# About 320 instructions at other places in the order of a Fourier-mixing and feed-forward kernel

## The chip, the cores and the metric

The kernel runs on one core of a Trainium2 chip. The metric is the device time of one execution in microseconds (us). The kernel before has a median of 676.51 us over three runs (675.86 to 678.52). Engines are named as in the profile: PE is TensorE, DVE is VectorE, ACT is ScalarE, POOL is GpSimd and SP is SyncE, which here only issues transfers.

## The reference

```python
a = einsum("bsd,ed->bse", LN(x), dft_hid_re);  b = einsum("bsd,ed->bse", LN(x), dft_hid_im)
h = x + einsum("ts,bse->bte", dft_seq_re, a) - einsum("ts,bse->bte", dft_seq_im, b)
out = h + silu(LN(h) @ w1) @ w2
```

Everything is float32, with batch 1, sequence length S = 2048, model width D = 512 and inner width F = 1792. LN subtracts the mean over the model width and divides by the root of the variance plus 1e-5.

## The kernel before

**Arithmetic.** A float32 product is made of three matmuls in the reduced format fp32r. Each moving operand is split by `rounded` (L236 to L250): ScalarE copies it to a high part `ph` (L242), and VectorE subtracts that from the source and has the remainder `pl` (L246, or L248 where a sign is turned). `three` (L290) then issues the products high by high, high by remainder and low weight by high (L292, L293, L294). All matmuls of the large stages take 512 columns. On top of this, the matrix products are done in forms with seven block products in place of eight, so VectorE also adds and subtracts blocks of the operands (`sub` and `prep`, L694; the results in L717, L790 and L840).

**Stages, in order of time.** The mixing along the sequence comes first, as the product of the sequence matrices with x: `plain(0,0)` (profile names c, X, S; up to about 98 us), `fast(1,0)` (m; to 165), then the mixing along the width, `mix(0)` (y; to 209), for the first half of the rows. Then the second half: `fast(0,1)` (m; to about 290), `fast(1,1)` (to 365) and `mix_fast(1)` (y; to 404), whose weights hf are read back from DRAM: they were stored there as fd and ad by GpSimd. The feed-forward layer follows, `down` and `up` (y, vx, g, f, wf, sf), until 670. In between VectorE and ScalarE make sums of w1 and w2 (`sums_w1`, L1051 to L1073; `make_w2`, L1174 to L1194), which are stored to DRAM and read back.

**The second layer norm.** h lies with the model width on partitions, so its mean and variance are sums over partitions. `total` (L956) adds the two tiles of h (L959), folds the result (L960), and calls GpSimd's `partition_all_reduce` (L961); this is the "sum over partitions". `norm_h` (L964) uses it twice for each of four blocks of rows: mean, centering (L976), squares on ScalarE (L982), variance. The variance then takes a trip through DRAM to be spread over 128 partitions of 4: a store of 2 KB from GpSimd (`row`, L988, `tk<-v`), a read (`gather`, L993, `rs<-tk`), twelve small operations on VectorE that make one over the root (`root` and `finish`, from L996), a store (L1002), a broadcast read (`spread`, L1005). The scaling L1010 follows, and the store nd (L1015), which the feed-forward stage reads back as hn.

**What sets the order.** `program` (L224) lists pieces of work, here called events, each with a time in us on a model clock. `step` puts a group of matmuls at the clock and its preparations at fixed leads ahead of it; `at` puts single pieces. Events are numbered in the order in which the code lists them. The last statement sorts them, and here the table MOVED (L44 to L132) comes in: it gives an offset in us to the event of a number.

```python
def step(n, mm, before=(), after=()):
    t, end = clock[0], clock[0] + n * MM_US
    for lead, f in before:
        events.append((t - lead, 1, len(events), f))
    events.append((t, 2, len(events), mm))
    ...
return sorted(((t + MOVED.get(n, 0.0), at, n, f) for t, at, n, f in events), key=lambda v: v[:3])
```

`fnet_ffn_kernel` goes through the sorted list twice. The first time it only notes when each SBUF page of 4 KB a partition is taken and last used, and `Plan.places` gives each tile one of 51 places, always the one that by its model has been free longest. The second time it emits the instructions and holds each of the five engines to exactly this order. So all engines work in order, SyncE's and GpSimd's transfers included: an instruction that waits holds back whatever stands behind it on its engine. A tile that takes a place also waits for the last users of the place, a store's landing among them.

**The events that the text names.** Each event here is written as its number.

- 369: matmuls of `mix(0)` (y, H10), before the next group. 376 and 389: loads of h from in_xT (L784), two halves each. 378: the first add h = y + h (L790), for which the matmuls of 425 wait. 380: the four sums hs of the second mixing matrix (L806).
- 431, 435, 440, 427, 448, 444: high parts on ScalarE; their remainders on VectorE are 432, 436, 441, 428, 449, 445. In the same way 462, 466, 470, 474, 498, 521, 551, 656, 664 are remainders of stage m; 477 is a sum of raw blocks (L694).
- 394 and 399: mean and variance of the first block of rows (two adds and the reduce each).
- 416 and 417: `root` and `finish` of the second block; 413, 414, 415 are its variance, `row` and `gather`.
- 684, 689, 694, 705, 710, 721: loads of hf for `mix_fast(1)` (two halves each); 686, 690, 696, 707 are the matmuls that read the first four. 695: a load of h from in_xT for the add L840 at 385 us. 825 to 828: loads hn<-nd.

Of the kernel before, what the change touches and what calls it, by code (L numbers as in the profile page):

```python
# [45 lines left out]
    12: 25.37, 14: 18.68, 16: 23.49, 21: 2.24, 24: 5.1, 28: 5.71, 30: 7.61, 31: 5.41, 32: 6.75, 35: 4.85, 36: 5.08,  # L46
    38: -0.24, 39: 3.5, 40: 6.36, 41: 1.55, 42: 0.25, 46: 6.79, 48: 5.99, 49: 5.67, 50: 7.6, 52: 3.63, 53: -4.14,
    54: -3.75, 57: -12.95, 58: -5.94, 59: 1.25, 60: -5.22, 61: -1.51, 63: 5.5, 64: -0.99, 65: -1.09, 66: -2.09,
    67: -0.1, 68: -0.57, 69: -14.93, 71: -24.64, 72: -18.25, 73: -16.87, 74: -15.18, 76: -0.67, 78: -10.64, 79: -6.28,
    80: 0.77, 81: -13.68, 82: 4.24, 84: -21.06, 85: -10.81, 86: -13.29, 87: -10.28, 88: 2.24, 89: 1.74, 92: -10.56,  # L50
    93: -1.15, 95: -6.14, 96: 3.53, 97: 1.06, 98: -1.97, 99: -0.07, 100: 2.76, 102: 0.43, 104: -2.79, 107: -8.69,
    108: -26.49, 110: -14.81, 111: -25.35, 112: -9.3, 116: 11.02, 118: 0.67, 119: 0.78, 121: 7.29, 122: 5.12,
    123: 9.89, 126: 0.66, 127: -0.06, 129: 5.4, 130: 4.42, 131: 1.43, 132: -0.74, 134: 0.06, 135: 0.91, 137: -2.02,
    138: -29.74, 139: -9.64, 141: -2.52, 142: 1.4, 145: -0.73, 146: -3.2, 147: -5.13, 148: -4.71, 149: 3.43,
    150: 2.26, 151: 19.19, 152: -27.16, 153: -17.66, 155: 11.15, 156: 11.07, 157: 17.67, 158: 17.63, 159: 14.66,
    160: 28.77, 161: 25.8, 162: -2.9, 163: -3.39, 164: -1.57, 165: -6.08, 166: -8.22, 167: 1.79, 168: -0.32,
    169: -3.29, 170: 3.74, 171: 1.24, 172: -18.88, 173: -19.39, 174: -6.33, 175: -8.5, 176: -5.26, 178: -5.15,
    179: -6.23, 180: 10.12, 181: 25.57, 182: -9.29, 183: -2.31, 184: 0.88, 185: 3.16, 186: 1.11, 188: 7.51, 189: 8.76,
    190: 7.03, 191: 5.95, 192: -10.95, 193: -3.24, 194: 8.07, 195: 6.17, 196: 5.36, 197: -18.74, 198: -10.39,
    199: -13.03, 200: -11.78, 201: -10.15, 202: 21.78, 203: 12.22, 204: 24.11, 205: 25.08, 206: 23.81, 207: -6.82,  # L60
    208: -5.87, 209: 5.68, 211: 0.38, 212: 4.81, 213: 4.09, 215: -5.32, 216: -0.23, 217: 2.38, 219: -16.42, 220: 5.22,
    221: 3.05, 223: 10.17, 224: -45.37, 225: -0.53, 226: 4.81, 228: -3.03, 229: 1.98, 230: 6.64, 233: 0.33, 234: 4.63,
    236: -20.67, 237: -4.86, 238: 4.99, 240: 13.91, 241: -7.64, 242: -8.45, 243: -2.11, 245: -18.15, 246: -15.09,
    247: -13.55, 249: -6.13, 250: -0.11, 251: 4.03, 253: -1.71, 254: 3.79, 255: 5.2, 257: 2.94, 258: 2.67, 259: 0.5,
    260: 1.59, 261: 0.52, 262: 2.64, 263: -2.76, 265: 4.76, 266: 3.32, 268: 4.67, 269: 6.93, 271: 6.39, 272: 7.88,
    273: 0.53, 274: 5.4, 275: 6.15, 276: -4.5, 278: 6.09, 279: 5.88, 280: 2.15, 282: 7.93, 283: 6.61, 285: 0.49,
    286: 0.9, 288: 2.33, 289: 2.31, 290: 2.16, 291: 2.6, 292: 2.43, 293: -5.69, 295: 3.01, 296: 5.2, 297: 6.85,
    299: -1.02, 302: -1.88, 303: 2.15, 305: 3.89, 306: 2.84, 307: 4.94, 308: 6.65, 309: 5.48, 310: -1.13, 312: 2.89,
    313: 6.78, 314: 5.19, 315: 2.32, 317: -4.12, 318: -0.55, 320: 3.15, 321: 1.08, 322: 2.71, 324: 2.35, 325: 6.97,
    326: 5.14, 327: 7.74, 329: 2.18, 330: -8.74, 331: 0.45, 332: 2.59, 333: 7.04, 334: 5.42, 335: -4.49, 338: 4.22,  # L70
    339: -12.19, 341: -15.7, 342: -18.67, 343: 1.36, 344: 2.27, 345: -2.79, 346: 2.6, 347: 2.51, 349: -4.7,
    350: -8.47, 351: -8.67, 352: 5.03, 353: 4.15, 354: -8.94, 355: 5.74, 356: 3.9, 357: 2.04, 358: -10.25, 360: -8.8,
    361: -4.61, 362: 0.81, 363: -0.42, 364: -0.7, 365: -1.32, 367: -4.56, 368: -3.92, 370: -9.58, 371: -5.5,
    372: -1.35, 373: 1.07, 374: -4.23, 375: -2.53, 376: 10.74, 378: 1.53, 379: 21.82, 380: -2.37, 381: -4.43,
    382: -1.85, 383: 9.92, 384: 12.54, 385: -3.96, 386: 19.12, 387: -5.64, 388: -2.68, 389: 6.11, 391: 2.25,
    392: 31.21, 393: 0.94, 394: -3.65, 395: -5.08, 396: -0.67, 397: 0.45, 398: -2.83, 399: -3.69, 400: -4.78,
    401: 3.37, 402: -1.34, 403: 0.17, 404: 5.79, 405: 8.49, 406: 2.76, 407: 6.66, 408: -27.67, 409: -5.26,
    410: -16.78, 411: -4.87, 412: -13.16, 413: -9.84, 416: 8.66, 417: 7.28, 418: 6.58, 419: 9.04, 420: 3.27,
    421: 8.16, 422: -3.11, 423: -3.82, 424: 0.47, 426: -23.77, 427: 3.56, 428: 6.96, 430: -16.19, 431: -11.09,
    432: -4.29, 434: -62.45, 435: 5.72, 436: 5.45, 439: -9.52, 441: 0.73, 444: -6.34, 445: -2.57, 447: -24.54,  # L80
    448: 2.95, 449: 2.53, 451: 1.94, 452: 3.93, 453: 5.93, 455: 11.48, 456: -5.77, 457: 6.32, 458: 6.74, 460: 5.56,
    461: 7.28, 462: 7.53, 464: 5.91, 465: 6.89, 466: 7.05, 468: -5.85, 469: -1.48, 470: 4.72, 472: -2.37, 473: -2.75,
    474: -1.83, 475: 0.43, 477: -0.58, 478: -2.17, 480: 1.69, 481: -0.48, 484: 6, 486: 5.62, 487: 5.35, 488: 5.34,
    489: 4.77, 490: 5.95, 491: 6.35, 493: 2.22, 494: 2.29, 495: -3.07, 497: -1.61, 498: 5.03, 500: 5.02, 501: 3.02,
    503: 5.25, 504: 4.47, 505: 1.31, 506: 1.52, 507: 2.32, 510: 6.63, 511: 5.94, 512: 9.73, 514: 5.45, 515: 5.04,
    517: -0.39, 518: 7.97, 520: 8.23, 521: 6.1, 522: 1.82, 523: 4.52, 524: 5.7, 525: -3.12, 527: 8.59, 528: 5.79,
    529: 3.62, 530: 7.7, 536: 4.91, 537: 3.2, 539: 2.32, 540: 6.62, 541: 6.7, 542: 8.33, 544: 9.12, 545: -33.8,
    546: 4.76, 547: 1.6, 548: 26.61, 549: -27.35, 550: -18.8, 551: -16.59, 554: 4.38, 555: 4.21, 558: 3.97, 559: 4.8,
    561: -9.81, 562: -5.24, 563: -6.01, 566: -6.52, 567: 4.31, 568: 4.51, 570: -20.73, 571: 0.57, 572: 0.31,
    575: -0.89, 576: 0.73, 578: -0.15, 579: 4.17, 580: 2.07, 582: 12.19, 583: 5.44, 584: 2.64, 585: 4.63, 587: -12.47,  # L90
    589: 2.94, 591: -11.64, 592: -5.78, 593: -7.73, 596: 6.89, 597: 5.63, 600: -3.91, 601: 3.55, 602: -6.54,
    603: -2.43, 604: -1.8, 605: -13.08, 607: -7.33, 608: 6.06, 610: -7.3, 614: 4.59, 615: -5.2, 616: -5.83,
    618: -8.39, 620: 8.96, 621: 7.18, 622: 6.56, 624: -1.21, 625: 3.84, 627: -8.97, 628: 5.64, 632: -4.62, 633: -5.73,
    634: -5.8, 635: -9.76, 637: 4.48, 638: 2.54, 639: 1.47, 642: 3.21, 644: 1.24, 645: 0.76, 647: -3.29, 648: -3.25,
    649: -12.3, 650: -8.36, 651: -1.12, 652: -19.86, 654: 3.38, 655: 3.83, 656: 2.17, 659: -14.33, 660: -13.59,
    663: -13.13, 664: -2.74, 666: 2.38, 667: 1.59, 668: 1.24, 669: 8.46, 672: -17.88, 673: -15.11, 674: -23.93,
    675: -34.26, 676: -17.44, 678: -28.28, 680: -19.6, 681: -3.67, 682: -8.48, 683: -1.66, 684: -18.81, 685: -5.98,
    687: -4, 688: -6.17, 692: -19.67, 693: -16.11, 694: 2.89, 695: 2.99, 697: 4.07, 698: 4.26, 699: -41.78, 701: 5.24,
    702: 4.58, 703: 4.51, 704: 7.6, 705: 3.1, 706: 17.25, 708: 1.9, 709: 1.31, 710: 2.94, 713: 1.55, 714: -20.76,
    716: -42.49, 717: -7.52, 719: -2.44, 721: -9.87, 723: 15.38, 724: -16.97, 728: 5.47, 730: 1.07, 731: 10.4,  # L100
    732: -3.37, 733: -0.27, 738: 12.29, 739: 13.87, 740: -42.3, 741: -31.4, 743: 2.11, 746: 4.55, 747: 9.34,
    748: 16.67, 749: 13.34, 750: 20.58, 751: 26.94, 752: 24.39, 753: 22.79, 754: 22.53, 755: 21.55, 756: 21.49,
    757: 26.94, 758: 47, 759: 32.53, 760: 38.11, 761: 39.91, 762: 13.17, 763: 13.96, 764: 16.64, 765: 14.1,
    766: 18.58, 767: 16.64, 768: 15.06, 769: 14.19, 770: 16.25, 771: 13.78, 772: 14.65, 773: 42.57, 774: 14.63,
# [1316 lines left out]
```

## Time and profile before

| | before |
|---|---|
| median of 3 runs | 676.51 us (675.86 to 678.52) |
| the profiled execution | 675.96 us |
| its span in the trace | 674.2 us |
| mean granted clock of TensorE in the span | 1.00 of full speed |
| matmuls (with 12 of warm-up) | 2916 |
| VectorE's share of busy time from 200 to 225, 225 to 250, 250 to 275 us | 0.82, 0.93, 0.98 |
| transfers | 189.59 MB, mean 281 GB/s |

The profile is one execution. Timeline rows give the start in us from the start of the span, the duration in us, the engine, the source line, the operation, output and inputs with tile shapes, and, in square brackets, how long the engine had been idle before and what ended that. Where rows of one kind follow each other they stand together as "x2" with the time of both. Rows of waits give what was waited for: us in total, times, longest. Rows of windows give the stretch, its length, the busy time of PE, PEld (weight load), DVE, ACT and POOL with counts, the granted clock, the busy share of the DMA engines and GB/s. Rows of transfers give the issuing queue, the count, the size of one, and the median us from issue to landing. Matmuls are pipelined, so one that takes 0.39 us in the trace is followed by the next after about 0.23.

### The profile page before, as it was taken

What the parts mean: (1) busy time and instruction counts of PE and PEld (TensorE: products, weight loads), DVE (VectorE), ACT (ScalarE), POOL (GpSimd) and SP (SyncE); (2) the same over time, 40 slices, a digit from 0 to 9 for tenths busy, and PEclk for the clock granted to TensorE, in tenths of its full rate; (3) what the DMA queues carried; (4) which work ended last, traced back from release to release, by engine and by line L of the source; (5) the groups of instructions that cost most, each with busy time, mean ns of one, the idle gap of its engine ahead of it and who ended that gap; (6) DMA issues with size and microseconds to landing.
All of it is one profiled execution on the core that took longest, in us unless ns stands there. A gap on an engine that the chain in (4) does not pass through costs nothing.

```text
span 674.2 us, 8332 instructions
## 1 busy us (share of the span) xinstructions
PE 666.1 (99%) x2916; PEld 545.9 (81%) x2916; DVE 576.0 (85%) x723; ACT 364.8 (54%) x459; POOL 99.0 (15%) x130
## 2 busy tenths in 40 slices
PE   9999999999999999999999999999999999999997
PEld 6878888888887788788888888888888888888886
DVE  7999999889868999889999998988989755568954
ACT  6987755544444544355554655666654555555700
POOL 0012210111211441303120002540200000000000
PEclk9999999999999999999999999999999999999999
DMA  8978897988799897798989988836998926788702
GB/s 319 398 187 266 231 395 267 320 281 254 281 347 349 291 350 207 216 351 318 343 268 362 412 300 307 311 126 232 343 373 321 352 87 234 256 291 295 280 31 94
DMA packets 61786, 189.59 MB, mean 281 GB/s; under 512 B 6960, under 2 KB 14640, under 8 KB 61744
## 3 DMA queue, kind: packets, MB, share of 16 engines
q1 hardware_dynamic: 46608, 136.33, 56.2%
q0 software_dynamic: 14848, 52.46, 24.1%
q8 instruction: 23, 0.38, 0.2%
q10 hardware_dynamic: 288, 0.26, 0.1%
q14 instruction: 19, 0.16, 0.1%
HBM read 142.88 MB, written 46.15 MB: 280 GB/s over the span
## 4 chain that ended last, share of the span: by engine, by line
PE 63%; DVE 1%; issue 1%; ACT 0%; DVEq 0%
PE f L294 6%; PE f L292 6%; PE f L293 6%; PE m L293 6%; PE m L294 6%; PE m L292 6%; PE y L293 6%; PE y L292 6%; PE y L294 6%; PE vx L292 3%; PE vx L294 3%; PE vx L293 3%; DVE pl L246 1%; PE f4b L294 0%; PE f4b L293 0%
## 5 line engine op out<-in xcount | busy, mean ns | idle before, releaser
L242 ACT ACTIVATE ph<-raw 128x1024 fp32r<-128x1024 f32 x102 | 105.0, 1057 | 95.5 <-DVE raw L694 19.5
L246 DVE TENSOR_TENSOR pl<-raw,ph 128x1024 fp32r<-128x1024 f32 x92 | 116.2, 1285 | 9.4 <-ACT ph L242 8.6
L293 PE MATMUL m<-pl,S 128*128 128x512 f32 x192 | 74.8, 390 | 1.0 <-DVE pl L248 1.0
L294 PE MATMUL m<-ph,S 128*128 128x512 f32 x192 | 74.7, 389 | 0.0
L292 PE MATMUL m<-ph,S 128*128 128x512 f32 x192 | 74.7, 389 | 0.0
L292 PE MATMUL f<-gth,wf 128*128 128x512 f32 x161 | 62.6, 389 | 0.0
L293 PE MATMUL f<-gtl,wf 128*128 128x512 f32 x161 | 62.6, 389 | 0.0
L294 PE MATMUL f<-gth,wf 128*128 128x512 f32 x161 | 62.6, 389 | 0.0
L242 ACT ACTIVATE gth<-g 128x1024 fp32r<-128x1024 f32 x42 | 42.9, 1052 | 29.8 <-DVE g L1237 21.3
L292 PE MATMUL m<-ph,X 128*128 128x512 f32 x144 | 56.2, 390 | 1.1 <-DVE h L790 1.1
L293 PE MATMUL m<-pl,X 128*128 128x512 f32 x144 | 56.3, 391 | 0.4 <-DVE pl L246 0.4
L294 PE MATMUL m<-ph,X 128*128 128x512 f32 x144 | 56.1, 390 | 0.0
L246 DVE TENSOR_TENSOR gtl<-g,gth 128x1024 fp32r<-128x1024 f32 x42 | 50.5, 1220 | 6.5 <-ACT gth L242 6.5
L1120 DVE TENSOR_TENSOR g<-vx,g 128x512 f32<-128x512 f32 x42 | 28.8, 688 | 31.0 <-PE vx L294 13.8
L694 DVE TENSOR_TENSOR raw<-raw,raw 128x1024 f32<-128x1024 f32 x36 | 43.9, 1221 | 0.6
L293 PEld LDWEIGHTS m<-pl,S 128*128 128x128 f32 x192 | 36.0, 188 | 8.8 <-DVE pl L248 1.4
L294 PEld LDWEIGHTS m<-ph,S 128*128 128x128 f32 x192 | 36.0, 188 | 7.5
L292 PEld LDWEIGHTS m<-ph,S 128*128 128x128 f32 x192 | 36.1, 188 | 7.5
L1117 ACT ACTIVATE g<-y 128x512 f32<-128x512 f32 x42 | 25.1, 596 | 29.6 <-PE y L294 29.3
L1114 ACT ACTIVATE g<-g 128x512 f32<-128x512 f32 x42 | 25.9, 627 | 19.6 <-DVE g L1120 19.5
L293 PEld LDWEIGHTS f<-gtl,wf 128*128 128x128 f32 x161 | 30.2, 188 | 6.3
L294 PEld LDWEIGHTS f<-gth,wf 128*128 128x128 f32 x161 | 30.2, 188 | 6.3
(334 smaller groups left out, 1581.2 us busy)
## 6 DMA issues: line engine op xcount, KB each, us to landing
raw<-in_seq SPq DMA_DIRECT2D x84, 512.0 KB, 6.7
wf<-wd SPq DMA_DIRECT2D x56, 512.0 KB, 5.4
sf<-sd SPq DMA_DIRECT2D x28, 512.0 KB, 5.5
raw<-in_seq POOLq DMA_DIRECT2D x16, 512.0 KB, 7.5
w<-in_ffn SPq DMA_DIRECT2D x28, 256.0 KB, 6.8
hf<-fd SPq DMA_DIRECT2D x12, 512.0 KB, 9.2
c<-cd SPq DMA_DIRECT2D x8, 512.0 KB, 8.0
h<-in_xT SPq DMA_DIRECT2D x8, 512.0 KB, 7.6
```

The lines of the kernel that those rows point to most:

```text
L242: nc.scalar.activation(hi, src, AF.Copy, scale=sign)
L246: nc.vector.tensor_tensor(lo, src, hi, op=ALU.subtract)
L292: nc.tensor.matmul(acc, wh, mh, start=first, stop=False, skip_group_check=on)
L293: nc.tensor.matmul(acc, wh, ml, start=False, stop=False, skip_group_check=on)
L294: nc.tensor.matmul(acc, wl, mh, start=False, stop=last, skip_group_check=on)
L694: nc.vector.tensor_tensor(o, a, b, op=ALU.subtract)
L1114: nc.scalar.activation(g[q, f][:, tau, :], src, AF.Silu)
L1117: nc.scalar.activation(g[q, f][:, tau, :], src, AF.Copy)
L1120: nc.vector.tensor_tensor(g[q, f][:, tau, :], src, g[q, f][:, tau, :], op=ALU.add)
```

## The change

The diff edits the table MOVED and nothing else. 260 offsets are altered and 33 are added; the values are in us on the model clock, and a more negative one puts the event earlier. No instruction is added, removed or resized. What changes is the order on VectorE, ScalarE, GpSimd and SyncE (TensorE's is the same), and the places of SBUF pages, which follow from the order. The lines with the events that the text speaks of:

```diff
-    376: 10.74, 378: 1.53, 379: 21.82, 380: -2.37, 381: -4.43,
-    382: -1.85, 383: 9.92, 384: 12.54, 385: -3.96, 386: 19.12, 387: -5.64, 388: -2.68, 389: 6.11, 391: 2.25,
+    376: 10.74, 378: 1.53, 379: 5.423, 380: -5.37, 381: -9.058, 382: -7.547, 383: 17.882, 384: 16.454, 385: -3.96, 386: 19.12,
+    387: -5.64, 388: -2.68, 389: 20.078, 391: 11.937, 392: 23.783, 393: -3.104, 394: -9.966, 395: -5.08, 396: -10.863,
...
-    416: 8.66, 417: 7.28,
+    414: -12.602, 415: -16.091, 416: -10.751, 417: -9.661,
...
-    435: 5.72, 436: 5.45, 439: -9.52, 441: 0.73, 444: -6.34, 445: -2.57,
+    435: -8.853, 436: -11.042, 438: 9.361, 439: -9.746, 440: -5.225, 441: -7.02, 444: 4.261, 445: 4.622,
...
-    464: 5.91, 465: 6.89, 466: 7.05, 474: -1.83, 477: -0.58, 498: 5.03, 551: -16.59,
+    464: -36.589, 465: -10.964, 466: -10.655, 474: 2.416, 477: 6.124, 498: -0.132, 551: 3.656,
...
-    684: -18.81, 694: 2.89, 705: 3.1, 710: 2.94,
+    684: -0.778, 689: -31.763, 694: -7.417, 705: -8.517, 710: -10.864,
...
-    50: 7.6, 57: -12.95, 58: -5.94, 99: -0.07,
+    50: 7.6, 57: -6.636, 58: 2.916, 99: -2.949,
```

(The entries of one line are put together here where the table has others between them.)

169 rows, old and new, of the table MOVED are left out of this document.

## The prediction

> **What bounds the kernel now.** I read the page's first part, then the view of what TensorE waits for, then busy time by stretch, then the timeline around each wait.
>
> ```profile
> span 674.2 us, 8332 instructions
> PE 666.1 (99%) x2916; PEld 545.9 (81%) x2916; DVE 576.0 (85%) x723; ACT 364.8 (54%) x459; POOL 99.0 (15%) x130
> ```
> ```profile
> PE m L292 <- DVE h L790: 1.1, 1, 1.1
> PE m L293 <- DVE pl L248: 1.0, 1, 1.0
> PE m L293 <- DVE pl L246: 0.4, 1, 0.4
> PE c L293 <- DVE pl L246: 0.2, 1, 0.2
> ```
> ```profile
> 200.00:225.00 25.00, 23.91 (x106) 19.48 (x105) 20.58 (x18) 10.38 (x12) 6.57 (x6) 1.00 0.86 320
> 225.00:250.00 25.00, 24.56 (x109) 20.02 (x108) 23.20 (x21) 13.09 (x16) 9.23 (x11) 1.00 0.97 344
> 250.00:275.00 25.00, 24.10 (x107) 19.62 (x105) 24.54 (x32) 10.51 (x10) 6.94 (x5) 1.00 0.67 191
> 400.00:500.00 100.00, 100.00 (x442) 82.79 (x442) 89.01 (x128) 58.70 (x86) 26.44 (x30) 1.00 0.75 275
> ```
>
> TensorE is the bound, at its full clock (1.00). 100 us hold 442 matmuls, so one starts every 0.226 us, and no part of this change takes a matmul away. All that can be won is in the places where that step is broken. These are the four rows of waits, 2.7 us in all, and three of them lie between 200 and 275. The price of each is read from start to start:
>
> ```profile
> 208.78 0.39 PE L294 MATMUL y<-ph,H11l 128*128 128x512 f32 x1
> 210.26 0.47 PE L292 MATMUL m<-ph,X 128*128 128x512 f32 x1 [1.09 <-DVE h L790]
> 234.89 0.39 PE L292 MATMUL m<-ph,X 128*128 128x512 f32 x1
> 235.72 0.50 PE L293 MATMUL m<-pl,X 128*128 128x512 f32 x1 [0.44 <-DVE pl L246]
> 273.71 0.39 PE L292 MATMUL m<-ph,S 128*128 128x512 f32 x1
> 275.09 0.50 PE L293 MATMUL m<-pl,S 128*128 128x512 f32 x1 [0.99 <-DVE pl L248]
> ```
>
> Less the normal 0.226, the gaps cost 1.25, 0.60 and 1.15 us. The first matmul after a wait is longer by some 0.1 (0.47 and 0.50 against 0.39), so the prizes are about 1.33, 0.72 and 1.27 us: 3.3 together. The wait in c gives 0.2 + 0.1, and steps too short for the waits view (estimate from the same start-to-start reading, over all matmuls) bring the total to about 5.0 us. That is the floor of the forecast: 0.74% of the time.
>
> **The change part by part.** It edits offsets in the order alone. No instruction goes or comes; TensorE's own order stays; on VectorE 165 of 720 instructions change place, on ScalarE 83, among SyncE's transfers 56, on GpSimd 19. The order also decides which freed pages of SBUF a tile takes, so some waits on a page's last user change too. Times below are those of before; S is what TensorE has gained by then.
>
> *The wait at 210 (−1.33).*
> ```profile
> 201.36 0.69 DVE L806 TENSOR_TENSOR hs<-hs,hid 128x512 f32<-128x512 f32 x1 [3.91 <-DMA fd<-hS01h]
> 208.89 2.36 DVE L790 TENSOR_TENSOR h<-y,h 128x1024 f32<-128x1024 f32 x2 [2.71 <-DMA h<-in_xT]
> 196.36 7.02 SPq L784 DMA_DIRECT2D h<-in_xT  x4
> h<-in_xT SPq DMA_DIRECT2D x4, 512.0 KB, 7.2
> ```
> TensorE waits for the add L790, and the add for a residual load (event 376) that SyncE issued late in its group of four, at 202.5, because it stood behind two others and waited for a store's page. In the new order it comes before them and waits only for the matmuls of event 369, which end near 198.3; issued there, with 7.2 us, it lands at 205.6. The add hS (380,2) no longer waits for the store either. Into the two holes (3.91 and 2.71) go two remainders, events 436 and 441, at 1.14 start to start. My walk of the alternating ScalarE and VectorE steps (435, 436, 431, 432, 440, 441) puts the add's first half at 207.7 to 208.9; TensorE could take it at 209.0. I take the whole 1.33; bound 0.9.
>
> *The wait at 235.7 (−0.72).*
> ```profile
> 234.45 2.35 DVE L246 TENSOR_TENSOR pl<-raw,ph 128x1024 fp32r<-128x1024 f32 x2
> 238.58 4.40 DVE L246 TENSOR_TENSOR pl<-raw,ph 128x1024 fp32r<-128x1024 f32 x2
> 238.83 4.06 POOL L961 PARTITION_ALL_REDUCE v<-v  x1 [4.33 <-DVE v L960]
> ```
> The remainder that is late (462) has sums 477 and remainder 474 (1.14 to 1.23 each) taken from in front of it, and 466 goes before the first reduce; one more operation in front leaves 1.23 net, twice the 0.60. New here is a page: remainder 445 waits for a store that landed at 220.75, with ten operations queued behind it. That store too is issued about 3 us earlier, and 445 has until 224.24 − S. I take the whole prize.
>
> *The wait at 275 (−1.0).*
> ```profile
> 249.26 1.23 DVE L246 TENSOR_TENSOR pl<-raw,ph 128x1024 fp32r<-128x1024 f32 x1 [1.49 <-ACT ph L242]
> 269.50 4.40 DVE L246 TENSOR_TENSOR pl<-raw,ph 128x1024 fp32r<-128x1024 f32 x2
> 269.75 4.06 POOL L961 PARTITION_ALL_REDUCE m<-m  x1 [6.30 <-DVE m L960]
> 273.82 1.21 DVE L248 SCALAR_TENSOR_TENSOR pl<-raw,ph 128x1024 fp32r<-128x1024 f32 x1
> ```
> Two remainders that take 2.35 elsewhere take 4.40 beside the reduce, so a reduce costs VectorE 2.05 us. In the rows the first of the pair keeps its 1.13 step and the second ends with the reduce. The late remainder (521) is the one behind them. Remainder 551 (1.14) goes behind it and 498 into the hole of 1.49: 2.6 us at best, 1.14 if the hole stays. TensorE needs 1.15. Gain 0.85 to 1.27; I take 1.0.
>
> [...]
>
> *The wait at 40 (+0.28).*
> ```profile
> 41.38 1.28 DVE L332 BATCH_NORM_STATS2 st<-x 128x6 f32<-128x512 f32 x2
> 36.84 0.30 DVE L333 BATCH_NORM_AGGREGATE mv<-st 128x2 f32<-128x6 f32 x2
> ```
> One statistics call (1.28 and half of 0.30, 1.41 with overlap) moves ahead of the remainder that TensorE waits for at 40.38, and one remainder (1.13) moves behind: 0.28 lost.
>
> *Small steps (−0.2).* One operation fewer in front at 73, two fewer before the reduce at 306: about 0.15 and 0.07.
>
> *The token chain of the second variance (0; −0 to +1.3).*
> ```profile
> 310.76 0.50 POOL L988 DMA_DIRECT2D tk<-v  x1 [0.29 <-POOL v L961]
> 318.65 0.88 POOL L993 DMA_DIRECT2D rs<-tk  x1
> 336.37 0.16 DVE L996 TENSOR_SCALAR rs<-rs 128x4 f32<-128x4 f32 x1
> ```
> The twelve small operations from L996 (2.2 us) move twenty places forward, to about 319.7. Their data come by two transfers on GpSimd's queue; the read now goes ahead of the raw load that stood before it. With the reduce 2.4 earlier and 4.5 us a hop (the store's median here) it lands at 317.5; with the 8.7 that the read took behind the raw load, at 321.6, and VectorE stands still 1.9 us with remainders behind it that have 0.6 to spare.
>
> *The late residuals of the last mixing stage (+0.3; 0 to +3).*
> ```profile
> 352.54 2.36 DVE L246 TENSOR_TENSOR pl<-raw,ph 128x1024 fp32r<-128x1024 f32 x2
> hf<-fd SPq DMA_DIRECT2D x8, 512.0 KB, 9.3
> DMA to landing us min/median/max: 6.0/9.2/10.6
> hf<-ad SPq DMA_DIRECT2D x2, 256.0 KB, 6.1
> 364.91 0.39 PE L292 MATMUL y<-ph,hf 128*128 128x512 f32 x1
> 385.12 1.22 DVE L840 TENSOR_TENSOR h<-61_3301,h 128x1024 f32<-128x1024 f32 x1
> ```
> Load 684, read by the matmul at 364.91, goes ten places later in SyncE's order, behind both halves of 694, and takes the page of remainder 664, which ends at 354.9. Issued at 355 to 355.6, it lands at 361 (6.1) to 364.9 (9.3; the third row is of all hf loads, 10.6 at most): a margin of 0 to 3.8. The remainder 656 at 352.54 also gets one more operation in front than leaves, against 0.5 us to spare and a hole of 1.1. Behind 684 the queue goes on: a load of h (695) waits for the landing of hn<-nd, which waits for the store nd; I get 384.4 for an add at 385.12, whose successors allow 1.2 more.
>
> *Everything else (0).* The W1 sums moved ahead between 130 and 200 fill holes of VectorE in front of remainders that were early. From 400 on hardly anything moves and TensorE is busy 100.00 of 100. If that cover failed, each us late would be one us.
>
> Sum: −1.33 − 0.72 − 1.0 + 0.28 − 0.2 + 0.3 = −2.7 us. The profiled execution took 675.96, 0.55 under the median of the runs, 676.51. So 673.3 there, 673.8 on the median.
>
> **Rivals.**
> A, nothing visible: holes filled at one seam push other remainders late by as much, as VectorE is busy 23.20 and 24.54 of 25 from 225 to 275. For: remainders behind the seams often have 0.5 us to spare. Against: the filled holes (3.91 and 2.71) lie ahead of the busy stretch. Of 3.0 at the seams 0 to 1.5 stays: 675 to 677.
> B, slower: load 684 and the chain on SyncE's queue behind it. It decides when 684 lands after 364.9 − S; each us more is one of TensorE's, and the next (690, 696, 707) follow at 2.7 us intervals, so a slide is paid once. A landing of 15 us, with the chain to the add at 385 as late again, gives 676.5 − 3.0 + 5 + 2 = 680.5. Against: no hf row shows over 10.6. 677 to 681.
> C, better: both start-up waits and the short steps close too: 676.5 − 4 = 672.5; floor 671.5.
> [...]
> That the order does not do what it says is shut out: the instruction lists differ as described.
>
> [...]
>
> **How the numbers follow.** Forecast 0.50 (672.4 to 675.2), A 0.18, B 0.14, C 0.12, D 0.06. 0.5%, or 3.4 us, is about what a measurement of this kernel can tell from no change: faster means under 673.1, slower over 679.9. Faster: C's 0.11 and 0.4 of the forecast's, 0.31. Slower: the upper half of B and what I have overlooked among 323 moved instructions, 0.15. Same 0.54. Range 671.7 to 677.8: C within, half of B without.
>
> **What would show it.** Right: the add h at 208 to 209 without a wait, and rows of waits at 235 and 275 gone; pl at 40 later by 0.3. TensorE's waits total under 1 us. Wrong: a row "PE y L292 <- DMA hf", a VectorE hole before L996 near 319 or before L840 near 385, or a wait of TensorE for a remainder that ends with a reduce.

## The result, and the profile after

The changed kernel has a median of 675.06 us over 22 runs (674.33 to 675.97). The kernel before, now also with 22 runs, has 676.96 us (674.14 to 678.52). The ratio is 0.9974, with a 95% interval of 0.9967 to 0.9982: 1.8 us faster, clear of the noise, and about half of the 0.5% that the prediction asks for before it says faster. The forecast was 673.8 us, a gain of 2.7. One execution of all in this study, of the kernel with three exchanges below, took 741.15 us at a granted clock of 0.85; the ratio given there is without it.

The page of the changed kernel, its first part:

```profile
span 672.9 us, 8320 instructions
PE 665.9 (99%) x2916; PEld 546.4 (81%) x2916; DVE 571.9 (85%) x723; ACT 364.6 (54%) x459; POOL 99.0 (15%) x130
```

The span is 1.3 us shorter, and VectorE is busy 4.1 us less. No work was taken from it: instructions with two SBUF inputs last longer beside a reduce (up to 3.26 us where 1.22 is usual), and fewer of them stand beside the last four. What TensorE waits for, in the changed kernel (us in total, times, longest):

```profile
PE m L300 <- DVE pl L255: 0.8, 1, 0.8
PE c L300 <- DVE pl L253: 0.4, 2, 0.3
PE vx L300 <- DVE T7l L253: 0.3, 1, 0.3
```

All lines are 7 higher than before. The rows for the add h (1.1) and for the remainder at 235 (0.4) are gone, the one at 275 is still there, and a new one stands in the feed-forward stage. TensorE's timeline around what is left:

```profile
208.98 0.39 PE L301 MATMUL y<-ph,H11l 128*128 128x512 f32 x1
209.47 0.47 PE L299 MATMUL m<-ph,X 128*128 128x512 f32 x1
...
272.14 0.39 PE L299 MATMUL m<-ph,S 128*128 128x512 f32 x1
273.31 0.50 PE L300 MATMUL m<-pl,S 128*128 128x512 f32 x1 [0.79 <-DVE pl L255]
...
402.42 0.39 PE L299 MATMUL vx<-T7h,sf 128*128 128x512 f32 x1
403.06 0.50 PE L300 MATMUL vx<-T7l,sf 128*128 128x512 f32 x1 [0.25 <-DVE T7l L253]
```

From here on the price of a wait is its gap from start to start less 0.226, plus what the next gap is too long, as in the prediction. That makes 0.35 at 209, 1.06 at 273 and 0.53 at 403. The table has the same for the two traces of each kernel, at the places in the order of work (times as in the kernel before); a dash is under 0.1, and the last column is the start of the last matmul.

| trace | 34 | 40 | 51 | 210 | 235 | 275 | 376 | 403 | 407 | elsewhere | last matmul |
|---|---|---|---|---|---|---|---|---|---|---|---|
| before | 0.47 | 0.28 | - | 1.33 | 0.72 | 1.27 | 0.22 | - | - | 0.15 at 73 | 669.56 |
| before, second trace | 0.31 | 0.28 | - | 1.23 | 0.87 | 1.26 | 0.19 | - | - | 0.19 at 73, 0.87 at 233 | 670.29 |
| after | 0.44 | 0.55 | 0.35 | 0.35 | - | 1.06 | - | 0.53 | 0.12 | 0.10 at 538 | 668.30 |
| after, second trace | 0.60 | 0.55 | 0.40 | 0.35 | - | 1.06 | - | 0.67 | 0.12 | 0.10 at 538 | 668.53 |

So in the first traces the gain is 0.98 at 210, 0.72 at 235, 0.21 at 275, and some 0.5 in small gaps at 18, 73, 311 and 376; lost are 0.27 at 40, 0.35 at 51, 0.65 at 403 and 407 and 0.10 at 538. TensorE's last matmul starts 1.26 us earlier; the rest of the sum is in steps too short for the table. The wait at 51 is new in the changed kernel:

```profile
51.06 0.39 PE L299 MATMUL c<-ph,X 128*128 128x512 f32 x1
51.52 0.50 PE L300 MATMUL c<-pl,X 128*128 128x512 f32 x1
```

Why 275 stayed is seen on VectorE. Its timeline in the changed kernel, and one row of ScalarE:

```profile
250.63 2.36 DVE L253 TENSOR_TENSOR pl<-raw,ph 128x1024 fp32r<-128x1024 f32 x2 [1.68 <-ACT ph L249]
...
262.32 1.23 DVE L253 TENSOR_TENSOR pl<-raw,ph 128x1024 fp32r<-128x1024 f32 x1 [1.27 <-ACT ph L249]
263.47 2.48 DVE L701 TENSOR_TENSOR raw<-raw,raw 128x1024 f32<-128x1024 f32 x2
...
267.72 1.22 DVE L701 TENSOR_TENSOR raw<-raw,raw 128x1024 f32<-128x1024 f32 x1
268.86 3.26 DVE L253 TENSOR_TENSOR pl<-raw,ph 128x1024 fp32r<-128x1024 f32 x1
272.05 1.21 DVE L255 SCALAR_TENSOR_TENSOR pl<-raw,ph 128x1024 fp32r<-128x1024 f32 x1
```
```profile
261.23 1.06 ACT L249 ACTIVATE ph<-raw 128x1024 fp32r<-128x1024 f32 x1 [1.43 <-PE m L300]
```

The hole of 1.49 at 249 was not filled; it is 1.68 now. Event 498 runs ahead of it, at 245.46, and not in it. The row names ScalarE, but the high part was ready at 249.87; a matmul that reads the page's earlier tile ends at 250.55, and the remainder (494) starts at 250.63. A second one of 1.27 has opened at 261: remainder 515 waits for its high part, and ScalarE could not make that before TensorE gave a page of SBUF back (the last row's releaser is a matmul). Remainder 551 did go behind, 1.14 us, but the second hole took it. The remainder that TensorE waits for (last row of the first fence) is the third behind the fold of the sums, after one that the reduce stretches to 3.26.

### The profile page after: what moved, and what is told of

Same layout as the page of the kernel before. It is cut to its first block, busy times and chain, and to the rows that moved or that the text cites. A ratio compares the mean times of both kernels' runs of the same rounds, so it can differ in the third digit from the quotient of the medians.

```text
span 672.9 us, 8320 instructions
## 1 busy us (share of the span) xinstructions
PE 665.9 (99%) x2916; PEld 546.4 (81%) x2916; DVE 571.9 (85%) x723; ACT 364.6 (54%) x459; POOL 99.0 (15%) x130
## 4 chain that ended last, share of the span: by engine, by line
PE 78%; DMA 9%; DVE 8%; issue 3%; ACT 1%; SPq 0%; DVEq 0%; ACTq 0%
PE m L300 7%; PE m L299 7%; PE m L301 7%; PE f L301 6%; PE f L300 6%; PE f L299 6%; PE y L300 6%; PE y L301 6%; PE y L299 6%; DMA raw<-in_seq 4%; PE vx L300 3%; PE vx L301 3%; PE vx L299 3%; PE c L300 2%; PE c L301 2%
## 5 line engine op out<-in xcount | busy, mean ns | idle before, releaser
L253 DVE TENSOR_TENSOR pl<-raw,ph 128x1024 fp32r<-128x1024 f32 x92 | 118.2, 1308 | 9.3 <-ACT ph L249 8.7
```

Of the source, the lines that this page charges most:

```text
L253: nc.vector.tensor_tensor(lo, src, hi, op=ALU.subtract)
```

## The experiments

### Half of the change alone

Offsets of the change for the events up to about 247 us, 153 of 293; the others as before.

> The offsets of the change for the events up to about 247 us (153 of 293), those of before for the rest. If the seams are separate, this keeps the whole of the early gain: the wait at 210 is 0.3 us long, the one at 235 is gone, the one at 40 is 0.55 us, and no wait stands at 403 us. Whether the wait at 275 (1.27 us before, 1.06 after, counted start to start with the longer matmul behind it) comes back to 1.27 tells how much of it the later half of the change took. The time should be 675.0 us or a little less against the 676.96 of before: the late half gave 0.21 + 0.29 and lost 0.53. Rival: the early gain is given back further on, since VectorE meets the same holes earlier; then new waits appear between 250 and 400 us and the time is that of before.

It took 676.83 us against 677.03, ratio 1.0001 (0.9987 to 1.0015): in the median nothing is left of the gain. The trace is that of the slowest of the ten executions, 678.57 us (the others 675.21 to 678.37). In it the prices at 40 (0.55), 210 (0.35) and 235 (none) are those of the changed kernel, so the early gain was there. It was lost at once, on TensorE's timeline, the clock beside it by windows (the third last number):

```profile
251.62 0.49 PE L294 MATMUL m<-ph,S 128*128 128x512 f32 x1 [0.99 <-ACT ph L244]
253.07 0.73 PE L295 MATMUL m<-pl,S 128*128 128x512 f32 x1 [0.96 <-DVE pl L250]
253.60 0.63 PE L296 MATMUL m<-ph,S 128*128 128x512 f32 x1
```
```profile
253.00:256.00 3.00, 2.93 (x7) 2.35 (x8) 2.93 (x4) 0.00 (x0) 0.89 (x1) 0.53 0.99 343
```

VectorE and ScalarE had both stood idle, 5.30 and 4.04 us, for a raw load of GpSimd (event 495). It was issued at 240.86, in the changed kernel at 240.78, but landed at 249.46 in place of 246.10. Load 549, which lies across the cut and keeps its place of before, is issued here at 235.0 and in the changed kernel at 254.0; that it is the one that slowed 495 was not tried. After the two waits TensorE ran at half clock for eight steps of 0.43 us, and the place cost 4.1 us in all. The early half by itself is therefore no gain. The rival was right that it is given back; in this trace its reason (the same holes) was not the cause. How much of the 4.1 us an execution at the median has is not shown, as the fastest of the ten is 3.4 us quicker than this one.

### The load at 210 by itself

The kernel before, with the second pair of residual loads moved behind the first:

```diff
-    389: 6.11,
+    389: 12.804,
```

> The kernel before with one event moved: the residual loads 389 go behind the second one of 376, so that the late half of 376 is issued when the matmuls of 369 end (198.3) and not at 202.5. VectorE's order is untouched; some waits on freed pages change with it. Theory: the load was the last to arrive at the wait of 210 us; landing at about 205 it is out of the way, the add follows the remainder that ends at 206.2, and the wait of 1.33 us goes: 675.2 to 675.6 us. Rival: VectorE's order has to change as well (the add hS waits until 201.36 for a store), and the wait stays above 0.3.

It took 675.83 us against 677.10, ratio 0.9980 (0.9966 to 0.9993), a little above the time expected. SyncE issued the load at 198.46, it landed at 206.09, and the add stands right behind the remainder hS10l:

```profile
204.77 1.22 DVE L246 TENSOR_TENSOR pl<-raw,ph 128x1024 fp32r<-128x1024 f32 x1
205.91 1.22 DVE L246 TENSOR_TENSOR hS10l<-hs,hS10h 128x1024 fp32r<-128x1024 f32 x1
207.04 2.35 DVE L790 TENSOR_TENSOR h<-y,h 128x1024 f32<-128x1024 f32 x2
```

The wait at 210 is gone altogether, though VectorE still stood 4.72 us for the store ahead of hs. So the load was the cause, and its place on SyncE's queue is the cure. Of the 1.33 us 0.49 came back at the next tight remainder, at 218 us. In the changed kernel 0.35 stays at 210, as the two remainders put in front of the add push its end to 209.33, past TensorE's 209.21; here, with nothing put in front, there is no wait.

### The wait at 275: a hole, or the reduce

Two exchanges in the changed kernel, each of two VectorE instructions. Neither changes the place of any tile in SBUF.

```diff
-    522: 6.406,
+    522: 6.399,
```

> The changed kernel with one pair of VectorE instructions exchanged: a sum of raw blocks (event 522) goes in front of a remainder (515), no other wait is altered. Theory: the wait at 273 us is what it is because VectorE stood idle 1.27 us at 261 us, where the high part for 515 waits for an SBUF page that TensorE frees at 261.19. With 522 (1.15 start to start) in that hole everything behind it is 1.15 earlier, the reduce starts at about 266.8, the remainder 521 ends at about 272.1, and TensorE, which needs it at 272.36, does not wait: 1.06 us less, 674.0 us. Rival: the partition reduce and the high part behind it set the moment alone (the raw sum 524 and ScalarE's 520 follow it), and the wait at 273 stays at 1.0.

It took 674.15 us, ratio to before 0.9953 (0.9935 to 0.9970). The sum 522 now lies in the hole (second row), and the late remainder ends 1.1 us earlier:

```profile
258.74 2.48 DVE L253 TENSOR_TENSOR pl<-raw,ph 128x1024 fp32r<-128x1024 f32 x2
261.13 1.22 DVE L701 TENSOR_TENSOR raw<-raw,raw 128x1024 f32<-128x1024 f32 x1
262.48 1.22 DVE L253 TENSOR_TENSOR pl<-raw,ph 128x1024 fp32r<-128x1024 f32 x1
...
270.94 1.21 DVE L255 SCALAR_TENSOR_TENSOR pl<-raw,ph 128x1024 fp32r<-128x1024 f32 x1
```

The wait of 1.06 us is gone. But 0.41 came at 292 and 0.45 at 374.

```diff
+    533: 0.768,
```

> The changed kernel with two remainders exchanged: 521, for which TensorE waits at 273 us, goes ahead of 533, which TensorE needs some 6 us later. 533 now is the instruction that a partition reduce stretches from 1.2 to 3.26 us. Theory (the stretched instruction in front is the cause): 521 itself is stretched, but ends with the reduce at about 272.1 in place of 273.26, and the wait of 0.95 plus 0.11 us is gone or under 0.1: 674.0 us. Rival (VectorE is late by its total work): whichever goes first, the later ones are late by as much, and a wait of about 1 us shows at the next remainder, 529 or 533, at 276 to 279 us: 675.0 us.

It took 674.52 us, ratio 0.9959 (0.9943 to 0.9974). The wait is gone here too. The late remainder is the first row, stretched, and the one that was stretched before follows:

```profile
270.89 1.97 DVE L255 SCALAR_TENSOR_TENSOR pl<-raw,ph 128x1024 fp32r<-128x1024 f32 x1 [1.21 <-ACT ph L249]
272.78 2.35 DVE L253 TENSOR_TENSOR pl<-raw,ph 128x1024 fp32r<-128x1024 f32 x2
```

No wait shows at 276 to 279; 0.48 shows at 374. Both cures work, so neither the hole nor the reduce is the cause alone: the remainder is late by their sum, and it is enough to take 1.1 us from the hole or to put the remainder ahead of the other one beside the reduce.

The reduce's part by itself: for this one sum the reduce covers 256 columns, and the rest of the means are left as the add put them.

> The changed kernel in which one partition reduce, that of the mean of the second block of rows (268 us), covers 256 of its 512 columns; the other half of the row of means is left with the values that the add put there. Theory: VectorE's instruction beside a reduce waits until shortly before the reduce's end; with a reduce of about 2 us in place of 4.06 the stretched remainder takes 1.2 to 1.4 in place of 3.26, VectorE is some 2 us earlier, and the wait at 273 us is under 0.15 in place of 1.06. Rival: the wait is set by pages and by ScalarE, and stays.

One run took 674.50 us. GpSimd's and VectorE's rows:

```profile
268.30 2.62 POOL L968 PARTITION_ALL_REDUCE m<-m  x1 [6.07 <-issue]
```
```profile
269.18 2.12 DVE L253 TENSOR_TENSOR pl<-raw,ph 128x1024 fp32r<-128x1024 f32 x1
```

The remainder is stretched by 0.90 in place of 2.04, and the wait at 273 is gone: 1.14 us taken from the reduce are enough too. No wait shows at 374; 0.34 shows at 387. The stretch had been guessed too small (0 to 0.2): the remainder ends 0.38 us behind this reduce, and 0.08 behind the whole one.

### Every reduce in two halves

```diff
-        nc.gpsimd.partition_all_reduce(t[:, 1, :], t[:, 0, :], channels=P, reduce_op=REDUCE_ADD)
+        for w in (slice(0, 256), slice(256, 512)):
+            nc.gpsimd.partition_all_reduce(t[:, 1, w], t[:, 0, w], channels=P, reduce_op=REDUCE_ADD)
```

> The changed kernel in which every partition reduce is issued as two, over 256 columns each; the result is the same. In the run with one reduce over half the columns the reduce took 2.62 us in place of 4.06 and stretched its remainder to 2.12 in place of 3.26: 0.90 over the normal 1.22 and not 2.04. Theory: what holds VectorE is in proportion to the columns (about 2.9 of 4.06 us, 1.4 of 2.62), and some 1.2 us at the end of each reduce are free; two halves then have two free ends, VectorE loses 0.9 to 1.8 us a reduce in place of 2.05, the wait at 273 us shrinks from 1.06 to between 0 and 0.8, and the time falls by 0.2 to 1 us to 674.1 to 674.9. Rival: the second half is held off by the VectorE instruction that runs in the free end, and holds the next one whole; VectorE loses 2 us or more a reduce, and the wait at 273 us and the time stay or grow.

It took 674.71 us, ratio 0.9966 (0.9956 to 0.9977). The two reduces of the mean at 268, and VectorE beside them:

```profile
267.80 4.65 POOL L969 PARTITION_ALL_REDUCE m<-m  x2 [5.06 <-issue]
```
```profile
268.68 2.12 DVE L253 TENSOR_TENSOR pl<-raw,ph 128x1024 fp32r<-128x1024 f32 x1
270.71 2.11 DVE L255 SCALAR_TENSOR_TENSOR pl<-raw,ph 128x1024 fp32r<-128x1024 f32 x1
272.75 1.21 DVE L253 TENSOR_TENSOR pl<-raw,ph 128x1024 fp32r<-128x1024 f32 x1
```

Two instructions are stretched by 0.90 and 0.90, so VectorE loses 1.80 in place of 2.05, and the wait at 273 falls from 1.06 to 0.82 (0.70 and 0.12): the poor end of what was expected. The time is at the edge of what can be told from the changed kernel.

### Three waits at a time

The hole filled, and the other two waits of the changed kernel cured in the same way:

```diff
-    99: -2.949, 522: 6.406, 731: 10.4,
+    99: -1.46,  522: 6.399, 731: 10.65,
```

> The changed kernel with three exchanges: 522 ahead of 515 as in the run before; the statistics call 99 behind the remainders 50 and 85 at 40 us; the add 731 behind the remainder 843 at 402 us. Theory: each of the three waits left in the changed kernel (1.06 at 273, 0.55 at 40, 0.53 at 403) goes by itself and nothing comes in its place: 2.1 us, 672.9 us, faster than both. Rival: VectorE has no room there, the waits move to the next remainder, and the gain is under 1 us.

It took 675.00 us, ratio 0.9964 (0.9953 to 0.9975), where 672.9 was expected: no faster than filling the hole alone. All three waits are gone, and others are there:

```profile
PE y L300 <- DVE T5l L253: 1.0, 1, 1.0
PE c L300 <- DVE pl L253: 0.7, 1, 0.7
PE y L300 <- DVE pl L253: 0.2, 1, 0.2
```

By gaps it is 0.94 at 51 in place of 0.55 at 40 and 0.35 at 51, and 1.27 at 407 in place of 0.53 at 403 and 0.12 at 407; 0.41 at 359 and 0.50 at 374 come on top. TensorE reached the next remainder earlier, and VectorE did not have it earlier: remainder 58 ends at 51.28 (51.47 in the changed kernel), T5l at 407.58 (407.27). The rival was right there: VectorE has no room at these two places, and only filling the hole brought something.

### The residual load that could have made it slower

Load 684 goes four issues later, behind 705 and 710; with it 39 tiles take another freed page of SBUF.

```diff
-    684: -0.778,
+    684: 2.86,
```

> The changed kernel with load 684 moved behind 705 and 710 on SyncE's queue, four issues later (from 351.2 to about 356.2 us). What my slower rival needed. Theory: SyncE's queue works in order, the load lands 10.1 us later as it did, at about 366.3, TensorE needs it at 362.98 and waits 3.3 us there; the following loads of the stage are earlier, so it is paid once: about 678 us, and 3.3 us of idle TensorE in one row. Rival: with the heavier load behind it the landing is quicker, or the wait is taken up by later slack, and the time grows by less than 1.5 us.

One run took 681.18 us. TensorE's timeline at the load, and the clock by windows:

```profile
367.24 0.77 PE L299 MATMUL y<-ph,hf 128*128 128x512 f32 x1 [3.69 <-DMA hf<-ad]
367.80 0.63 PE L300 MATMUL y<-pl,hf 128*128 128x512 f32 x1
368.23 0.63 PE L301 MATMUL y<-ph,hf 128*128 128x512 f32 x1
```
```profile
365.00:370.00 5.00, 2.76 (x7) 2.21 (x8) 4.33 (x4) 0.00 (x0) 0.00 (x0) 0.65 1.04 412
370.00:375.00 5.00, 5.00 (x17) 3.95 (x16) 0.00 (x0) 2.69 (x3) 0.53 (x1) 0.67 1.02 402
```

The load landed at 367.11, and the wait is paid once, as the theory had it. But it costs more than its length: after 3.85 us of gap, fourteen steps run at 0.43 to 0.56 in place of 0.226, which is 2.9 us more. Together that is 6.8, and the last matmul starts 6.5 us later than in the changed kernel.

### The kernel before once more

> The kernel before once more, for a second trace of it. The profiled execution of before took 675.96 us, 1.0 under its median of 676.96, and its trace shows 1.26 us more than that of the changed kernel from the first to the last matmul, where the medians differ by 1.90. Theory: before has remainders that are ready within 0.1 us of their need, so its waits vary from run to run, and this trace shows other small waits or longer ones than the first at the same places (210, 235, 275), 0.5 to 1 us more in all. Rival: the same waits to 0.05 us, and the missing 0.6 us lies outside the matmuls, at start or end.

One run took 676.69 us. The waits of the table are there again, and one more, for a remainder at 233 behind sums whose raw load was late:

```profile
227.92 3.75 DVE L694 TENSOR_TENSOR raw<-raw,raw 128x1024 f32<-128x1024 f32 x3 [1.21 <-DMA raw<-in_seq]
```

The last matmul starts 0.73 later than in the first trace of before, within what was expected. So the trace on which the prediction was made is a good one of its kernel.

### The best of these, beside the changed kernel

The hole filled and the reduces split, the hole alone again, and the changed kernel again, on one chip with before at 676.95 us.

> The run with the hole filled (522 ahead of 515) and every reduce in two halves. Filling the hole took away the wait of 1.06 us at 273, but 0.45 came back at 374 us, behind the stretch from 300 to 350 in which VectorE was busy 24.55 and 24.85 of 25 us. Theory: with less of VectorE lost to the reduces the wait at 374 shrinks from 0.45 to under 0.2, and the time is 0.2 to 0.5 us under that of the hole alone. Rival: as for the split alone.

> The hole alone once more (522 ahead of 515), beside the changed kernel on the same chip: 0.5 to 1.0 us faster than it. In its first trace 0.41 of the 1.06 us came back at 292, where a load landed 2.5 us later than in the other traces, and 0.45 at 374; if the first is chance, it is missing here, and the second stays.

> The changed kernel itself, for a second trace and a time on the same chip: the waits of the first trace at 40, 209, 273 and 403 us within 0.1 us, 1.3 to 2 us under before.

| kernel | median us | ratio to before (95% interval) | 40 | 51 | 210 | 275 | 374 | 403 | last matmul |
|---|---|---|---|---|---|---|---|---|---|
| changed | 675.12 | 0.9975 (0.9964 to 0.9986) | 0.55 | 0.40 | 0.35 | 1.06 | - | 0.67 | 668.53 |
| hole filled | 673.99 | 0.9963 (0.9950 to 0.9975) | 0.44 | 0.40 | 0.34 | - | 0.39 | 0.74 | 667.54 |
| hole filled, reduces split | 673.87 | 0.9956 (0.9939 to 0.9974) | 0.55 | 0.39 | 0.34 | - | - | 0.76 | 667.20 |

The wait at 292 in the first trace of the filled hole is not there, which fits that run's late load as its cause. The wait at 374 is there both times, and it is gone in the one trace in which the reduces are split as well. Filling the hole is 1.1 us better than the changed kernel by medians in the same call, and the pair is 3.1 us better than before; the last two cannot be told from each other, where 0.2 to 0.5 us had been expected.

## Why the prediction was right, and where its sizes were off

*The bound.* TensorE had nothing to gain but its waits, and no trace shows any other gain.

*The wait at 210: forecast 1.33, bound 0.9, measured 0.98.* The cause was named rightly: the load alone takes the wait away. The walk of the alternating steps was some 0.4 us too short. ScalarE's high part 431 waits for the page of remainder 436, and VectorE stood 1.12 us for it:

```profile
205.65 2.54 DVE L253 TENSOR_TENSOR pl<-raw,ph 128x1024 fp32r<-128x1024 f32 x2 [1.12 <-ACT ph L249]
208.11 2.35 DVE L797 TENSOR_TENSOR h<-y,h 128x1024 f32<-128x1024 f32 x2
```

*The wait at 235: forecast 0.72, measured 0.72.* Remainder 462 now ends at 232.03, and 477 and 474 stand behind it, as the prediction has it; TensorE comes to it at 234.28. No run makes this move alone. Remainder 445's page, named as new, was no harm: the store landed at 215.99.

*The wait at 275: forecast 1.0, measured 0.21.* This is the term that was mis-sized most. The prediction put event 498 into the hole of 1.49 and, at worst, kept the hole. It looked at which instruction stands where and not at when the pages come free that the high parts and remainders take. The hole stayed, for a page that TensorE still held, and a second one of 1.27 opened for another; in this order both are freed by matmuls of the same stage. For the first, the page itself changed: in the kernel before remainder 494 took one that matmuls of event 482 freed (249.17), in the changed kernel one that those of 485 free (250.55), which by TensorE's progress, 1.55 us ahead by then, is 2.9 us later. The runs with the hole filled and with half a reduce show that 1.1 us of VectorE would have been enough.

*The statistics at 40: forecast +0.28, measured +0.27.* The remainder that moves behind is 58. The prediction counted what that frees at 40, and put at nothing what it costs at 51, where 58 is needed: it ends at 51.47 (39.20 in the kernel before), and TensorE loses 0.35.

*Small steps: forecast 0.2, measured 0.2* at 73 and 311; 0.1 at 18 and 0.2 at 376 came without having been named.

*The token chain: forecast 0, bound 1.3, measured 0.* The read was issued at 306.48 behind a hop of 2.6, landed at 311.01, and VectorE came to it at 316.07 without a hole.

*The late residuals: forecast +0.3, bound 3, measured 0.* Load 684 was issued at 351.18 and landed at 361.31, 1.7 us before TensorE's 362.98. It was issued as remainder 664 ended (351.15), as the prediction has it. At 10.1 us it took longer than the 6.1 to 9.3 that I had reckoned with; the issue was 4 us earlier than my walk, as VectorE was ahead (664 ended at 354.90 before). That the two errors cancelled was luck. The rival that hung on it was priced by its wait alone, 5 us for 5. The run with the late load shows the full price, 6.8 us for 3.69 of idle time; 2.9 of them are the clock's, which was granted at 0.65 from 365 to 370 and at 0.67 from 370 to 375.

*From 400 on: forecast 0, measured +0.65.* "Hardly anything moves" was wrong for VectorE between 388 and 405: remainder 834 comes ten places earlier, ahead of T7l, and 741 twenty-eight later, into the same stretch. The prediction did not walk it. That these two moves make T7l late is read from the order; the run with three exchanges shows only that VectorE has no room there.

*Sum and base.* The terms give 2.7; the first traces show 1.26, the second trace of each 1.76, the medians 1.90. The sum was made against an execution 1.0 us under the median of before. Its weak point is that the trace of before, like any, shows one draw of the transfers: the second has 0.87 at 233 that the first lacks. The changed kernel's runs lie within 1.6 us, those of before within 4.4. The measured 675.06 us lies at the upper end of the forecast (672.4 to 675.2) and at the lower end of rival A (675 to 677), so the time alone does not decide between them. The terms do in part: of 3.05 us forecast at the three seams 1.91 came, where A gave 0 to 1.5, but what A describes, remainders made late elsewhere, is what was seen at 51 and 403. Of the signs named, the add at 208 to 209, the missing row at 235 and the 0.3 at 40 came; the row at 275 did not go, and TensorE's waits add up to 1.5 us and not to under 1. None of the signs of being wrong came.

*VectorE beside a reduce.* A two-input instruction over 128x1024 that starts during a reduce of 512 columns ends 0.07 to 0.09 us behind it, in the traces of both kernels; less its usual 1.22 us, that is 1.13 to 1.15 ahead of the reduce's end. The profile calls its spans on GpSimd rough, so when exactly VectorE is free again is not shown. D among the prediction's chances is a reduce that costs VectorE 1.2 us more than the 2.05 read from the trace of before; no run shows that term: in the changed kernel the remainder beside the reduce at 268 takes 3.26, which is 2.04 over its 1.22. An instruction whose other input is PSUM shows no such stretch in the changed kernel:

```profile
417.47 3.23 POOL L968 PARTITION_ALL_REDUCE m<-m  x1 [3.35 <-DVE m L967]
```
```profile
418.99 0.69 DVE L1127 TENSOR_TENSOR g<-vx,g 128x512 f32<-128x512 f32 x1 [1.19 <-ACT g L1124]
```

It begins inside the reduce and takes 0.69, which is the median of all 42 of its line. This, too, is why the last four reduces cost VectorE less than before: four such instructions begin inside them, where it was one. The four reduces hold two-input instructions back by 1.78, 1.74, 0.39 and 1.74 us before, and by 0.17 and 1.66 after, which makes most of the 4.1 us.

## What to carry to other kernels

Where one engine is busy 99% and a second almost so, a cured wait is worth its length only if the second engine has a hole to give it from; look ahead for the next stretch where that engine is full (here 300 to 350, 24.56 and 24.82 us of 25) and expect the echo behind it. In an order with few buffers, walk the freed buffers along with the instructions: the holes that decided this case were waits for a page. And make the sum on more than one trace of before where remainders are ready within 0.1 us of their need.

## What the runs showed of the hardware that was not expected

TensorE's clock fell to half in two runs, in one of them after less idling than one long wait. In the run with the late load 3.69 us idle were followed by fourteen steps of 0.43 to 0.56. In the run of the early half two waits of 0.99 and 0.96 with one matmul between them were followed by eight slow steps, 1.7 us more than the waits themselves. The wait of 1.09 in the kernel before, alone, was followed by none.

Half clock lasts 3.41 us in the trace of the early half, from 253.16 to 256.57, and 6.83 us in that of the late load, from 366.50 to 373.33. The 3.41 us ahead of the fall and the slow ones in the trace of the early half, and a stretch as long in the kernel before that holds the wait of 1.09:

```profile
249.75:253.16 3.41, 1.47 (x6) 0.66 (x5) 2.51 (x3) 1.81 (x2) 0.55 (x1) 1.00 0.12 28
253.16:256.57 3.41, 3.41 (x8) 2.66 (x9) 3.34 (x3) 0.00 (x0) 0.89 (x1) 0.50 0.93 308
```
```profile
207.63:211.05 3.42, 2.33 (x11) 1.62 (x10) 2.16 (x2) 0.00 (x0) 0.42 (x1) 1.00 0.95 325
```

TensorE was busy 1.47 of 3.41 us in the stretch that was followed by half clock (0.47 in the run with the late load), and 2.33 in the one that was not. So in these three cases the fall goes with how little TensorE worked in the stretch, and not with the length of one wait. What happens between 1.47 and 2.33 no run shows.

A reduce of 256 columns takes 2.62 us and one of 512 takes 4.06 where a VectorE instruction with two SBUF inputs began 0.25 us ahead of it. With one ahead that has its other input in PSUM they take 1.79 (the first of the two below, in the run with all reduces in halves) and 3.23, in both cases 0.83 less:

```profile
417.48 3.56 POOL L969 PARTITION_ALL_REDUCE m<-m  x2 [3.06 <-DVE m L967]
```

What makes the 0.83 no run shows. The end in which VectorE is free again is not fixed either: by the reckoning above 1.14 us of a whole reduce (at 268 in the changed kernel), 0.84 of a half one (2.12 less 1.22, in the run with half a reduce). The expectation for the halves had taken 1.2 for both, and two halves saved only 0.24 of 2.04 us a reduce.
